# The routing of a fused attention and two-MoE kernel: dummy products, a mask in one step, and the slots' one-hots in small steps on VectorE

## The chip, the cores and the metric

The kernel runs on one core of a Trainium2 chip. The metric is the device time of one execution in microseconds, the median of three runs. One further execution was taken by the hardware profiler; all times below that are read from a view are on its clock.

## The reference

Three stages follow one another:

```python
# 1. attention, 4 x 8 heads, 576 tokens, head size 64
scores = (q @ k.T) / 8
kth = np.partition(scores, -32, axis=-1)[..., -32:-31]
attn = softmax(np.where(scores >= kth, scores, -1e9))
x = (attn @ v) as 2304 x 512
# 2. soft MoE: 8 experts x 4 slots, hidden size 1024
logits = x @ phi
slot_input = softmax(logits, over tokens).T @ x            # 32 x 512
slot_out[e] = relu(slot_input[e] @ w1[e]) @ w2[e]          # 32 x 512
x = softmax(logits, over the 32 slots) @ slot_out          # c @ slot_out
# 3. noisy top-2 MoE: 8 experts, hidden size 1024
noisy = x @ w_gate + log1p(exp(x @ w_noise)) * noise
top2, top2_w = the two largest of noisy, softmax over the two
for e: mask = top2 == e
       out[mask] += top2_w * (relu(x[mask] @ u1[e]) @ u2[e])
```

## The kernel before, in words

The input of the third stage is never formed. A token's row is c, 32 numbers, times slot_out, so each expert's first layer is the token's c times a matrix g = slot_out @ u1[e] of 32 x 1024. g and c are held as two halves each (gh and gl, high and low part), stacked into 128 rows (`stacked_g`, L928).

What the change touches lies between the end of the soft MoE and the ninth of the 64 chunks of the third stage:

- *Logits* (up to L999). c is turned (five transposes on PE, two copies on ACT, the tile ct), and PE forms the logits of both gates from it. Meanwhile it forms g of expert 0 in four steps of `weigh01`.
- *Choice* (L999 to L1047). DVE adds the noise and takes the largest values of each token (MAX8, L1004, 18 of them). Two one-hots oh follow by comparison, and their sum is the mask mb (L1021). From it PE counts, for each token and expert, how many tokens stand before (`before` and onesb, L1027 and L1030). Between the mask and these, L1024 takes the high half of g from its sum on PE, so that ACT can read the low half (L1039). `gates` (L1044 to L1047) makes the weights of the two experts, puts them into RW, rows of 36 numbers (c, the token's id, the gate), and has SP write RW to DRAM: the transfer xd (L1048).
- *Compaction* (L1133 to L1170). Expert 0's tokens are gathered by PE: 18 one-hots wx, each made by DVE (L1143) or by two steps of ACT (L1140, L1141), times c. The steps of `weigh01` for expert 1 stand between these products. The result is cts.
- *Addresses* (L1072 to L1078). For each token its two places in the eight experts' lists: a partition and a column, pc.
- *Slots* (`spread`, L1084 on, and `rows_of_slots`). The lists are turned round by products of one-hots: 36 of 128 wide for the partitions (the tiles y) and 36 of 40 wide for the columns (eq, times ctn into cx and rr, and times pn). The partitions' one-hots of the first 24 are made by a subtraction on POOL (`far`, L1090) and by Abs and Relu on ACT (`near`, L1094, L1095), and those of the last 12 by DVE (`same`, L1099). 36 products on PE (L1120) give ridx, for every place of a list the row of xd, 40 numbers on each of 128 partitions.
- *Gathers.* By ridx POOL fetches an expert's rows out of xd (`rows`, L1218, five indirect transfers of 128 rows each). `ids_of` (L1223) takes the ids from them, `slots` (L1229 to L1231) and `turn` (L1237) make cts of the expert.
- *Chunks* (`gated`). Chunk n = 8e + c is an eighth of expert e's hidden size. `first(n)` is PE's product g times cts (L1249), its relu as a high half hh on ACT (L1254) and a low half hl on DVE (L1255). `split(n)` makes the halves wh and wl of u2 (L1262, L1265). `second(n)` is, for each of five groups of 128 tokens, three products into one bank (L1273 hh by wh, L1274 hh by wl, L1275 hl by wh). After chunk 7 of an expert `store` scales the five banks by the gate and POOL adds them into the output (L1286).

All engines take their instructions in the order in which the code issues them. Chunk n's loop body is: split(n+2), two groups of second(n), first(n+2), the other three groups, and then the extras of `if n == ...`. `later` (before chunk 8) folds a flag over the partitions, which tells whether the fast path may be trusted; its transposes are L697. SP issues the weights' transfers in one queue, as buffers come free. tb, gp, tl and t2 are pools of memory: tb (with RW in it) is given back before tl (the tiles hl) and t2 (the one-hots, cx, xs) are opened, and the memory of tl and t2 is laid out again over what came free.

Of the kernel before, what the change touches and what calls it, by code (L numbers as in the profile page):

```python
# [40 lines left out]
def moe_after_topk_attention(ctx: ExitStack, tc: tile.TileContext, q, k, v, phi, w1, w2, wg, wn, noise, u1, u2, qk, vt, out):  # L41
# [740 lines left out]
    def moe(st, xp, xs, fast):  # L782
# [26 lines left out]
        def warm(n):  # L809

            p = bank("acc0")
            for _ in range(n):
                T.matmul(p, onesb, onesb.unsqueeze(1).to_broadcast([128, 4, 128]), start=True, stop=True)
# [89 lines left out]
        ct = tb.tile([128, 5, 128], F32, name="ct")  # L903
        cf = cn.rearrange("p t s -> p (t s)")
        pc = [bank(x) for x in ("acc3", "acc2")]
        for g in range(4):
            T.transpose(pc[0][:, g * 128:g * 128 + 128], cf[:, g * 128:g * 128 + 128], identf)
        T.transpose(pc[1][:64, :128], cf[:, 512:576], identf)
# [45 lines left out]
        def halve1(e, p):  # L954
            for x, h, _ in quarters(e, p):
                A.copy(h, x)
            for x, h, l in quarters(e, p):
                V.tensor_tensor(l, x, h, op=OP.subtract)
# [58 lines left out]
        oh = gp.tile([128, 2, TT, 8], F32, name="oh")  # L1017
        V.tensor_tensor(oh, ng.unsqueeze(1).to_broadcast([128, 2, TT, 8]),
                        m8[:, :, 0:2].rearrange("p t c -> p c t").unsqueeze(3).to_broadcast([128, 2, TT, 8]), op=OP.is_equal)
        mb = small("mb", BF)  # L1020
        V.tensor_tensor(mb, oh[:, 0], oh[:, 1], op=OP.add)  # L1021
        V.tensor_tensor(gw[:, 1], m8[:, :, 1], m8[:, :, 0], op=OP.subtract)
        for r, (x, h, _) in enumerate(quarters(0, P0)):
            T.matmul(x, minus, h.bitcast(F32), start=False, stop=True, tile_position=(0, 32 * r), skip_group_check=True)  # L1024
# [8 lines left out]
        T.matmul(tot[:, :144], onesb, mbf, start=True, stop=True)  # L1033
        tots = SM
# [6 lines left out]
        A.activation(gw[:, 1], gw[:, 1], AF.Exp)  # L1041
# [38 lines left out]
        def spread(t2):  # L1080
# [6 lines left out]
            eq = t2.tile([128, 36, m], BF, name="eq", bufs=1)  # L1087
# [27 lines left out]
            return pairs, far, near, same, columns, partitions  # L1115
# [74 lines left out]
        gated(st, ps, halves, tw, gather, cts0, done, first_weights, halve1, keep_g, stacked_g, GSS, begin, later,  # L1190
# [3 lines left out]
    def gated(st, ps, halves, tw, gather, cts0, done, first_weights, halve1, keep_g, stacked_g, GSS, begin, later,  # L1194
# [107 lines left out]
        for n in range(8 * E):  # L1302
# [6 lines left out]
            if n < 8 * E - 4:  # L1309
# [3 lines left out]
                if n == 2:  # L1313
                    rows_of_slots(ps.tile([128, 512], F32, name="tp"), pairs)
# [47 lines left out]
            if e + 1 < E:  # L1362
                if c == 1 and e + 1 != 4:
# [154 lines left out]
```

## Time and profile before

| | |
|---|---|
| median of three runs | 760.02 us (758.58 to 761.44) |
| the profiled execution | 757.91 us, its span 756.1 us |
| mean granted clock of PE | 0.982 |
| busy: PE, its weight loads, DVE, ACT, POOL | 727.9, 602.4, 556.5, 489.0, 505.2 us |
| chain that ended last, by engine | PE 51%, DVE 25%, POOL 11%, issue 6%, DMA 4% |
| moved by DMA | 135.22 MB |

The span is the time from the first to the last instruction of the profiled execution; its own time lies 1.8 us above that. The attention fills the first half, with all engines busy. From about 450 us to the end PE is the busiest engine. The routing lies between 455 and 530 us.

### The profile page before, as it was taken

To read this page: it belongs to the slowest core of one execution; us is meant where nothing else is said; L and a number is where in the kernel's file an instruction comes from. 1 tells how busy PE (TensorE), PEld (TensorE's weight loads), DVE (VectorE), ACT (ScalarE), POOL (GpSimd) and SP (SyncE) were. 2 spreads that over 40 slices of the span, in tenths; PEclk is the share of its full clock that TensorE was granted. 3 is DMA by queue.
4 is the path that set the end of the run, shared out by engine and by line. 5 is a ranking of instruction groups with operands and counts; after the bars stand their busy time and mean duration, and the time that the engine had idled before them with its cause. 6 is when DMAs were issued, how large, how long until landed. Compare 5 with 4: busy or idle time off the path is not lost.

```text
span 756.1 us, 17319 instructions
## 1 busy us (share of the span) xinstructions
PE 727.9 (96%) x5654; PEld 602.4 (80%) x5654; DVE 556.5 (74%) x2632; ACT 489.0 (65%) x1025; POOL 505.2 (67%) x639
## 2 busy tenths in 40 slices
PE   9899999999999999999999997979999999999995
PEld 5799999898999889998889434657885888888884
DVE  7799999999999998999984414856654555555551
ACT  5799999999999999999997204634222222322221
POOL 5999999998999999999775030354742337254044
PEclk9899999999999999999999999989999999999999
DMA  7257869775776634463468699969783987245045
GB/s 210 70 129 212 229 175 241 192 219 159 214 219 186 156 107 105 105 156 74 112 235 300 218 379 395 301 231 322 175 185 92 335 249 146 44 68 74 2 64 70
DMA packets 63286, 135.22 MB, mean 179 GB/s; under 512 B 13650, under 2 KB 14290, under 8 KB 63186
## 3 DMA queue, kind: packets, MB, share of 16 engines
q1 hardware_dynamic: 56146, 123.84, 54.6%
q0 software_dynamic: 7040, 10.18, 9.8%
q8 instruction: 46, 0.75, 0.4%
q14 instruction: 54, 0.44, 0.2%
HBM read 84.37 MB, written 17.97 MB: 135 GB/s over the span
## 4 chain that ended last, share of the span: by engine, by line
PE 51%; DVE 25%; POOL 11%; issue 6%; DMA 4%; ACT 1%; SPq 0%; POOLq 0%; ACTq 0%
DVE c L498 10%; PE acc L1275 9%; PE acc L1273 9%; PE acc L1274 9%; POOL u L521 5%; PE av L562 5%; DVE TH L529 5%; DVE c L505 4%; PE S L462 3%; POOL s L536 3%; PE hp L1249 2%; PE st L541 2%; DMA wx<-in_moe_w_dram 2%; DVE mx L501 2%; PE acc L827 2%
## 5 line engine op out<-in xcount | busy, mean ns | idle before, releaser
L498 DVE MAX8 c<-s 128x8 f32<-128x82 f32 (+1 forms) x1008 | 227.0, 235 | 4.3 <-ACT s L478 3.2
L521 POOL TENSOR_TENSOR u<-g,s 128x576 f32<-128x576 bf16 x144 | 186.5, 1295 | 0.5 <-ACT g L515 0.5
L562 PE MATMUL av<-vb,et 128*128 128x65 f32 (+1 forms) x1600 | 172.3, 262 | 0.8 <-ACT et L548 0.8
L562 PEld LDWEIGHTS av<-vb,et 128*128 128x128 f32 (+1 forms) x1600 | 165.7, 180 | 7.8 <-issue 5.3
L1286 POOL DMA_INDIRECT out_dram<-y,ii x40 | 64.7, 1618 | 122.2 <-ACT y L1285 60.7
L1254 ACT ACTIVATE hh<-hp 128x640 fp32r<-128x640 f32 x62 | 43.8, 707 | 137.4 <-PE hp L1249 128.3
L1275 PE MATMUL acc<-wh,hl 128*128 128x512 f32 x320 | 127.0, 397 | 0.7 <-DVE hl L1255 0.7
L1273 PE MATMUL acc<-wh,hh 128*128 128x512 f32 x320 | 127.4, 398 | 0.0
L1274 PE MATMUL acc<-wl,hh 128*128 128x512 f32 x320 | 126.6, 395 | 0.0
L529 DVE MAX8 TH<-u 128x8 f32<-128x584 f32 x144 | 109.8, 763 | 18.8 <-POOL u L522 17.8
L536 POOL TENSOR_SCALAR s<-s,mx 128x576 f32<-128x576 f32 x144 | 108.1, 751 | 22.4 <-ACT a L535 13.6
L541 PE MATMUL st<-identf,s 128*128 128x128 f32 x576 | 116.3, 282 | 4.4 <-POOL s L536 3.9
L1255 DVE SCALAR_TENSOR_TENSOR hl<-hp,hh 128x640 fp32r<-128x640 f32 x62 | 51.1, 824 | 92.1 <-ACT hh L1254 86.7
L535 ACT ACTIVATE a<-s,TH 128x576 bf16<-128x576 f32 x144 | 117.5, 816 | 0.2
L515 ACT ACTIVATE g<-s,T 128x576 bf16<-128x576 f32 x144 | 116.6, 810 | 0.5 <-POOL u L521 0.5
L462 PE MATMUL S<-ks,qs 128*128 128x288 f32 x600 | 113.0, 314 | 0.0
L542 PE MATMUL st<-steep,a 128*128 128x128 bf16 x576 | 106.5, 220 | 0.0
L480 ACT ACTIVATE s<-S 128x576 f32<-128x576 f32 x141 | 97.0, 688 | 6.6 <-PE S L469 4.6
L541 PEld LDWEIGHTS st<-identf,s 128*128 128x128 f32 x576 | 84.3, 146 | 13.5 <-POOL s L536 6.5
L553 ACT ACTIVATE et<-st 128x512 f32<-128x512 f32 x144 | 90.4, 628 | 5.6 <-PE st L542 4.9
L462 PEld LDWEIGHTS S<-ks,qs 128*128 128x128 f32 x600 | 84.7, 190 | 2.0
L1275 PEld LDWEIGHTS acc<-wh,hl 128*128 128x128 f32 x320 | 60.6, 189 | 14.4 <-DVE hl L1255 1.2
(337 smaller groups left out, 1155.5 us busy)
## 6 DMA issues: line engine op xcount, KB each, us to landing
wa<-in_moe_w_dram SPq DMA_DIRECT2D x8, 2048.0 KB
wa<-in_moe_w_dram SPq DMA_DIRECT2D x28, 512.0 KB
wb<-in_moe_w_dram SPq DMA_DIRECT2D x5, 2048.0 KB
ks<-hl SPq DMA_DIRECT2D x60, 160.0 KB
ks<-raw SPq DMA_DIRECT2D x60, 160.0 KB
raw<-in_qk_dram SPq DMA_DIRECT2D x15, 608.0 KB
wy<-in_moe_w_dram SPq DMA_DIRECT2D x4, 2048.0 KB
wb<-in_moe_w_dram SPq DMA_DIRECT2D x16, 512.0 KB
```

Of the source, the lines that this page charges most:

```text
L462: T.matmul(ph[hf][:, :288], QS[h][:, q0:q0 + 128], KS[h][:, l, ks], start=(n == 0), stop=(n == len(mm) - 1))
L498: V.max(C[i][:, c * 8:c * 8 + 8], SS[i][:, cut[c]:cut[c + 1]])
L515: A.activation(g, SS[i], AF.Sign, bias=last8(T24, i, 1), scale=-OVER, accum_out=SM[:, i:i + 1])
L521: G.tensor_tensor(u[:, 0:S], G1[i], SS[i], op=OP.mult)
L529: V.max(last8(TH, i), UU[i])
L535: A.activation(AP[i // 2][:, S * (i % 2):S * (i % 2) + S], SS[i], AF.Relu, bias=last8(TH, i, 1), scale=-1.0)
L536: G.tensor_scalar(SS[i], SS[i], -1.0, MX[i][:, 0:1], op0=OP.mult, op1=OP.add)
L541: T.matmul(o, SP[i // 2][:, ks], identf, start=True, stop=True, is_transpose=True)
L562: T.matmul(av[h][o:o + m, tt * 65:tt * 65 + 65], x, VB[j % 2][:, h, c if c < 4 else 4 + i % 2], start=(c == 0), stop=(c == 4), tile_positi ...
L1273: T.matmul(ACC[j], HH[n][:, r], WH[n], start=(c == 0), stop=False)
L1274: T.matmul(ACC[j], HH[n][:, r], WL[n], start=False, stop=False)
L1275: T.matmul(ACC[j], HL[n][:, r], WH[n], start=False, stop=(c == 7))
```

## The change

The edits, in the order of the code:

- `turn_c` forms ct inside the loop over the experts of the soft MoE, before its last expert, not after the loop.
- Six products with no use (`warm(6, "acc2")`) follow the four steps of `weigh01(0)`.
- mb is one comparison with the second largest value, ahead of oh. The products of L1024 stand behind the counts.
- `gates` runs after the compaction. `addresses` runs in chunk 0, not ahead of it.
- The one-hots y of tokens 0 to 15 and 24 to 35 are 28 steps of DVE, each 128 x 128 on a 16-bit ramp ntb; those of tokens 16 to 23 are nine steps of ACT. ctn has a number for each place of eq and is 16-bit, and the product with it runs on DVE. POOL makes none of these. They are spread over chunks 0, 1 and 2.
- `rows_of_slots`, `rows(1)` and `ids_of(1)` stand after chunk 3 (before: within and after chunk 2), `first_weights2` after chunk 4 (before: chunk 3). The stacked g of expert 1 is written at chunk 3, not 1.
- `keep_tie`, three small steps of DVE ahead of the flag's fold in `later`, marks a tie of the two largest values.
- Some tiles are padded, so that the buffers behind them start elsewhere.

```diff
@@ the soft MoE's loop
             if e == E - 2:
+                turn_c()
                 A.copy(sos, sx)
@@ the logits
                 weigh01(0, c, P0)
+            warm(6, "acc2")
@@ the choice
+        V.tensor_tensor(mb, ng, m8[:, :, 1:2].to_broadcast([128, TT, 8]), op=OP.is_ge)
         V.tensor_tensor(oh, ...)
-        V.tensor_tensor(mb, oh[:, 0], oh[:, 1], op=OP.add)
-        V.tensor_tensor(gw[:, 1], m8[:, :, 1], m8[:, :, 0], op=OP.subtract)
-        for r, (x, h, _) in enumerate(quarters(0, P0)):
-            T.matmul(x, minus, h.bitcast(F32), start=False, stop=True, ...)
+        V.tensor_tensor(below, m8[:, :, 1], m8[:, :, 0], op=OP.subtract)
...
         T.matmul(tot[:, :144], onesb, mbf, start=True, stop=True)
+        for r, (x, h, _) in enumerate(quarters(0, P0)):
+            T.matmul(x, minus, h.bitcast(F32), start=False, stop=True, ...)
@@ the one-hots
-        ctn = gp.tile([128, 2 * TT], F32, name="ctn")
+        ctn = gp.tile([128, 2 * TT, E * JT], BF, name="ctn")
+        ntb = gp.tile([128, 128], BF, name="ntb")
...
-            def far(k):
-                G.tensor_tensor(lt[k], nt[:, 0:128].unsqueeze(1).to_broadcast([128, 8, 128]),
-                                pc[:, 0, 8 * k:8 * k + 8].unsqueeze(2).to_broadcast([128, 8, 128]), op=OP.subtract)
+            def far(a, b):
+                for i in range(a, b):
+                    V.tensor_scalar(lt[i // 8][:, i % 8], ntb, pc[:, 0, i:i + 1], None, op0=OP.is_equal)
             def near(k):
-                A.activation(lt[k], lt[k], AF.Abs)
+                for i in range(8):
+                    A.activation(lt[k][:, i], ntb, AF.Abs, bias=pc[:, 0, 8 * k + i:8 * k + i + 1], scale=-1.0)
                 A.activation(lt[k], lt[k], AF.Relu, bias=1.0, scale=-1.0)
...
-                    G.tensor_tensor(x[:, :, 0], eq[:, a:a + n], ctn[:, a:a + n].unsqueeze(2).to_broadcast([128, n, m]),
-                                    op=OP.mult)
+                    V.tensor_tensor(x[:, :, 0], eq[:, a:a + n], ctn[:, a:a + n], op=OP.mult)
@@ the compaction
-        for n, c in zip((3, 3, 3, 3), range(4)):
+        for n, c in zip((0, 3, 3, 3), range(4)):
             some(n)
             weigh01(1, c, P1)
...
-        some(2)
-        gates()
         some(TT)
@@ the flag
+        def keep_tie():
+            tie = gp.tile([128, 1], F32, name="tie")
+            V.tensor_reduce(tie, below, op=OP.max, axis=AX.X)
+            V.tensor_scalar(tie, tie, 0.0, None, op0=OP.is_lt)
+            V.tensor_tensor(sure, sure, tie, op=OP.mult)
         def later(t2):
+            keep_tie()
@@ the chunks
         gather()
-        addresses()
+        gates()
         done()
...
             if n == 0:
-                begin()
-                for k in range(3):
-                    far(k)
-                    near(k)
+                halve1(1, P1, False)
+                addresses()
                 columns()
                 partitions()
-                for k in range(3, 5):
-                    same(k)
+            if n == 1:
+                near(2)
+                far(0, 16)
             if n == 2:
+                far(24, 2 * TT)
+                halve1(1, P1, True)
+            if n == 3:
+                rows_of_slots(ps.tile([128, 512], F32, name="tp"), pairs)
                 rows(1)
                 ids_of(1)
-            if n == 3:
+            if n == 4:
                 first_weights2(ps.tile([128, 512], F32, name="tp"))
-            if n == 4:
                 slots(1)
                 rows(0)
```

How the instructions stand, at three places. Names: acc, hp and tp are banks of sums, gw the two gates, cts and hl as above, RW the rows that xd writes, zs the flag's tile. "waits" names the semaphores on which an instruction waits, by engine or by the lane of the transfers (DMAHW4 is a lane of SP's). A number behind a name is that of the buffer.

The first place is DVE, from the end of the compaction to the first hl. Before, where L1044 to L1047 stand ahead of three one-hots of the compaction (not shown), and L1072 to L1078 behind it:

```order
L1047 COPY RW<-gw 128x36 [waits DVE_49]
...
L1170 CAST cts_8730<-acc_8648 64x320 [waits PE_49]
L1170 CAST cts_8730<-acc_8648 64x320
L1072 TENSOR_TENSOR oh<-oh,pe 128x288 [waits DVE_49]
...
L1078 TENSOR_SCALAR pc<-ia 128x72 [waits DVE_49]
L1255 SCALAR_TENSOR_TENSOR hl<-acc_8761,hh 128x320 [waits Activation_49]
L1255 SCALAR_TENSOR_TENSOR hl<-acc_8762,hh 128x320 [waits Activation_49]
```

And now:

```order
L1172 CAST cts_8734<-acc_8657 64x320 [waits PE_49]
L1172 CAST cts_8734<-acc_8657 64x320
L1051 TENSOR_SCALAR gw<-gw 128x18
L1052 RECIPROCAL gw<-gw 128x18 [waits DVE_49]
L1053 TENSOR_TENSOR gw<-gw 128x18 [waits DVE_49]
L1054 COPY RW<-gw 128x36 [waits DVE_49]
L1262 SCALAR_TENSOR_TENSOR hl<-acc_8764,hh 128x320 [waits DMAHW4_49,DVE_49,Activation_49]
L1262 SCALAR_TENSOR_TENSOR hl<-acc_8765,hh 128x320 [waits Activation_49]
L1272 TENSOR_TENSOR wl<-wa_8447,wh 128x512 [waits Activation_49]
```

The gates moved behind the copies of cts, the addresses went to chunk 0, and the first hl has a wait on DMAHW4, the lane of xd, which it did not have. Before, the first to wait for that lane was POOL, in the first of these rows of its own queue; of them only the gathers of L1218 are left on POOL now:

```order
L1090 TENSOR_TENSOR y<-nt,pc 128x1024 [waits DMAHW0_49,DVE_49,DMAHW4_49,PE_49,DMAHW7_49,Activation_49,Pool_49]
L1090 TENSOR_TENSOR y<-nt,pc 128x1024 x2
L1106 TENSOR_TENSOR cx<-eq,ctn 128x16x40 [waits DVE_49,Pool_49]
L1106 TENSOR_TENSOR rr<-eq,ctn 128x20x40 [waits DVE_49]
L1218 DMA xs<-xd,ridx 128x36 [waits DVE_49]
```

The second place is ACT in chunks 0 to 2. Before:

```order
L1254 ACTIVATE hh<-hp 128x640 [waits PE_49]
L956 CAST gh_8512<-tp 32x256 x4
L1094 ACTIVATE y<-y 128x1024 [waits DMAHW4_49,Pool_49]
L1095 ACTIVATE y<-y 128x1024 [waits Activation_49]
...
L1111 ACTIVATE cx<-eq,pn 128x16x40 [waits DVE_49]
L1111 ACTIVATE rr<-eq,pn 128x20x40 [waits DVE_49]
L1262 CAST wh<-wa_8446 128x512
L1254 ACTIVATE hh<-hp 128x640 [waits PE_49]
```

And now:

```order
L1261 ACTIVATE hh<-hp 128x640 [waits PE_49]
L963 CAST gh_8511<-tp 32x256 x4
L1115 ACTIVATE cx<-eq,pn 128x16x40 [waits DVE_49,DMAHW4_49,Activation_49,Pool_49]
L1115 ACTIVATE rr<-eq,pn 128x20x40 [waits DVE_49]
L1269 CAST wh<-wa_8447 128x512
L1261 ACTIVATE hh<-hp 128x640 [waits PE_49]
L1104 ACTIVATE y<-ntb,pc 128x128 x8
L1105 ACTIVATE y<-y 128x1024 [waits Activation_49]
L1269 CAST wh<-wa_8447 128x512 [waits DMAHW5_49]
```

The six large steps on y went; the steps on eq now stand first, and eight small ones and one large one stand a chunk later.

The third place is PE before chunk 8, where the flag is folded. Before:

```order
L1274 MATMUL acc_8812<-wl,hh 128x512
L1275 MATMUL acc_8812<-wh,hl 128x512
L697 MATMUL tp<-identf,zs 1x128
L1273 MATMUL acc_9212<-wh,hh 128x512 [waits Activation_49]
L1274 MATMUL acc_9212<-wl,hh 128x512
```

And now:

```order
L1281 MATMUL acc_8815<-wl,hh 128x512
L1282 MATMUL acc_8815<-wh,hl 128x512
L697 MATMUL tp<-identf,zs 1x128 [waits DVE_49]
L1280 MATMUL acc_9251<-wh,hh 128x512 [waits Activation_49]
L1281 MATMUL acc_9251<-wl,hh 128x512
```

L697 stands where it stood, and now waits for DVE, on whose queue the steps of `keep_tie` come after the two products y of the store of chunk 7.

## Rows read from the trace of the kernel before

**Rows 1.** Windows: PE, PEld, DVE, ACT, POOL busy (count), PEclk, DMA share, GB/s

```profile
469.00:471.00 2.00, 1.21 (x4) 0.60 (x4) 2.00 (x6) 1.94 (x5) 0.00 (x0) 0.58 1.05 387
476.00:476.50 0.50, 0.50 (x7) 0.21 (x9) 0.50 (x2) 0.00 (x0) 0.00 (x0) 0.84 0.99 246
```

**Rows 2.** Timeline of PE: start, duration (us), instruction, [idle before it <- released by]

```profile
467.10 0.63 PE L1024 MATMUL acc<-gh,minus 32*32 32x256 f32 x8 [1.61 <-ACT gh L1015]
...
470.52 0.58 PE L1147 MATMUL acc<-wx,xw 128*64 128x320 f32 x2 [0.63 <-ACT wx L1141]
...
481.28 1.06 PE L1249 MATMUL acc<-cts,gs 128*128 128x320 f32 x4 [0.79 <-ACT cts L1169]
...
483.69 0.50 PE L1275 MATMUL acc<-wh,hl 128*128 128x512 f32 x1 [0.74 <-DVE hl L1255]
...
494.50 0.73 PE L1120 MATMUL tp<-cx,y 128*128 128x80 bf16 x16 [2.18 <-issue]
...
506.69 0.62 PE L1205 MATMUL tp<-wa,soT 128*32 128x512 f32 x1
...
510.26 0.50 PE L1273 MATMUL acc<-wh,hh 128*128 128x512 f32 x1
...
517.85 0.60 PE L1237 MATMUL tp<-identf,cx 128*128 128x128 f32 x4
...
526.90 0.38 PE L697 MATMUL tp<-identf,zs 128*1 128x128 f32 x2
```

**Rows 3.** Timeline of SP's queue, issues of transfers

```profile
470.56 0.53 SPq L132 DMA_DIRECT2D wa<-in_moe_w_dram  x1
477.56 0.35 SPq L1048 DMA_DIRECT2D xd<-RW  x1
```

**Rows 4.** POOL's line L1090: duration min/median/max (ns), first and last start (us)

```profile
L1090 POOLq EVENT_SEMAPHORE  x3: 43/43/25372, 457.9 to 484.3; - x3
```

**Rows 5.** Timeline of POOL

```profile
499.54 1.26 POOL L1218 DMA_INDIRECT xs<-xd,ridx  x1 [3.81 <-DVE ridx L1126]
...
508.13 0.19 POOL L1223 CAST ii<-xs 128x5 int32<-128x5 f32 x1 [2.09 <-DMA xs<-xd,ridx]
...
521.66 0.19 POOL L1223 CAST ii<-xs 128x5 int32<-128x5 f32 x1 [6.58 <-DMA xs<-xd,ridx]
```

**Rows 6.** Timeline of DVE

```profile
465.38 1.32 DVE L1004 MAX8 nz<-T 128x8 f32<-128x8 f32 x18
...
481.54 0.46 DVE L1072 TENSOR_TENSOR oh<-oh,pe 128x288 f32<-128x288 f32 x1
...
483.04 0.20 DVE L1078 TENSOR_SCALAR pc<-ia 128x72 f32<-128x72 int32 x1
483.16 0.88 DVE L1255 SCALAR_TENSOR_TENSOR hl<-acc,hh 128x320 fp32r<-128x320 f32 x2
...
486.86 0.81 DVE L1255 SCALAR_TENSOR_TENSOR hl<-hp,hh 128x640 fp32r<-128x640 f32 x1
...
515.16 0.36 DVE L1231 CAST cx<-cx 128x320 fp32r<-128x320 f32 x1
...
526.40 1.40 DVE L1283 TENSOR_SCALAR y<-acc,xs 128x512 f32<-128x512 f32 x2
```

**Rows 7.** Groups of DVE by form, 420 to 520 us: busy us, mean ns | idle

```profile
L958 DVE TENSOR_TENSOR gl<-tp,gh 32x256 fp32r<-32x256 f32 x4 | 1.7, 420 | 0.1
L1104 DVE TENSOR_TENSOR eq<-nt,pc 128x800 bf16<-128x800 f32 x1 | 1.0, 979 | 0.0
```

**Rows 8.** Groups of ACT by form, the same stretch

```profile
L1262 ACT CAST wh<-wa 128x512 fp32r<-128x512 f32 x8 | 4.9, 614 | 0.0
L1254 ACT ACTIVATE hh<-hp 128x640 fp32r<-128x640 f32 x6 | 4.2, 705 | 10.1 <-PE hp L1249 10.0
L1095 ACT ACTIVATE y<-y 128x1024 bf16<-128x1024 bf16 x3 | 3.2, 1058 | 0.1
```

**Rows 9.** Group of DVE by form, whole span

```profile
L64 DVE TENSOR_SCALAR before<-jp 128x128 bf16<-128x128 int32 x1 | 0.2, 223 | 0.0
```

More of the change, by code (lines that the diff above doesn't have):

```diff
@@ L807, in moe, with warm @@
         more(20)
-        def warm(n):
-            p = bank("acc0")
+        def warm(n, name="acc0"):
+            p = bank(name)
             for _ in range(n):
@@ L879, in moe, with turn_c @@
                             op0=OP.max)
+        ct = tb.tile([128, 5, 128], F32, name="ct")
+        def turn_c():
+            cf = cn.rearrange("p t s -> p (t s)")
+            x = halves()
+            for g in range(4):
+                T.transpose(x[:, 0, g * 128:g * 128 + 128], cf[:, g * 128:g * 128 + 128], identf)
+            T.transpose(x[:64, 1, :128], cf[:, 512:576], identf)
+            A.copy(ct[:, 0:4], x[:, 0].rearrange("p (a b) -> p a b", a=4))
+            A.copy(ct[:64, 4], x[:64, 1, :128])
         sx, so = bank("acc2"), [bank(f"acc{n}") for n in range(2)]
@@ L902, in moe @@
             more(19 if fast else 20)
[L903 to L908, printed above, removed]
         p = fold_t(sos, 4, fold)
-        A.copy(ct[:, 0:4], pc[0].rearrange("p (a b) -> p a b", a=4))
-        A.copy(ct[:64, 4], pc[1][:64, :128])
         ta_st.close()
         gp = pool("gp", 1, st)
-        soT = gp.tile([128, 4, NS], F32, name="soT")
+        soT = gp.tile([128, 4 * NS + 24], F32, name="soT")[:, 0:4 * NS].rearrange("p (c s) -> p c s", s=NS)
         V.tensor_copy(soT, p)
@@ L952, in quarters, with halve1 @@
                     for r in range(4)]
-        def halve1(e, p):
-            for x, h, _ in quarters(e, p):
-                A.copy(h, x)
+        def halve1(e, p, lo):
             for x, h, l in quarters(e, p):
-                V.tensor_tensor(l, x, h, op=OP.subtract)
+                if lo:
+                    V.tensor_tensor(l, x, h, op=OP.subtract)
+                else:
+                    A.copy(h, x)
         def keep_g(g):
@@ L1017, in moe @@
         oh = gp.tile([128, 2, TT, 8], F32, name="oh")
+        mb = small("mb", BF)
+        V.tensor_tensor(mb, ng, m8[:, :, 1:2].to_broadcast([128, TT, 8]), op=OP.is_ge)
         V.tensor_tensor(oh, ng.unsqueeze(1).to_broadcast([128, 2, TT, 8]),
                         m8[:, :, 0:2].rearrange("p t c -> p c t").unsqueeze(3).to_broadcast([128, 2, TT, 8]), op=OP.is_equal)
-        mb = small("mb", BF)
-        V.tensor_tensor(mb, oh[:, 0], oh[:, 1], op=OP.add)
-        V.tensor_tensor(gw[:, 1], m8[:, :, 1], m8[:, :, 0], op=OP.subtract)
-        for r, (x, h, _) in enumerate(quarters(0, P0)):
-            T.matmul(x, minus, h.bitcast(F32), start=False, stop=True, tile_position=(0, 32 * r), skip_group_check=True)
+        below = gp.tile([128, TT], F32, name="below")
+        V.tensor_tensor(below, m8[:, :, 1], m8[:, :, 0], op=OP.subtract)
         pos = bank("acc3")
@@ L1033, in moe @@
         T.matmul(tot[:, :144], onesb, mbf, start=True, stop=True)
+        for r, (x, h, _) in enumerate(quarters(0, P0)):
+            T.matmul(x, minus, h.bitcast(F32), start=False, stop=True, tile_position=(0, 32 * r), skip_group_check=True)
         tots = SM
@@ L1040, in moe @@
         stacked_g(0)
-        A.activation(gw[:, 1], gw[:, 1], AF.Exp)
+        A.activation(gw[:, 1], below, AF.Exp)
         def gates():
@@ L1114, in spread @@
             pairs = [(lt[i // 8][:, i % 8], r[i]) for i in range(2 * TT)]
-            return pairs, far, near, same, columns, partitions
+            return pairs, far, near, columns, partitions
         def rows_of_slots(p, pairs):
@@ L1189, in done, with gated @@
             xs.close()
-        gated(st, ps, halves, tw, gather, cts0, done, first_weights, halve1, keep_g, stacked_g, GSS, begin, later,
+        gated(st, ps, halves, tw, gather, cts0, done, first_weights, halve1, keep_g, stacked_g, GSS, P1, gates, later,
               addresses, spread, rows_of_slots, ridx, soT, gh, gl)
-    def gated(st, ps, halves, tw, gather, cts0, done, first_weights, halve1, keep_g, stacked_g, GSS, begin, later,
+    def gated(st, ps, halves, tw, gather, cts0, done, first_weights, halve1, keep_g, stacked_g, GSS, P1, gates, later,
               addresses, spread, rows_of_slots, ridx, soT, gh, gl):
@@ L1294, in gated @@
         gather()
-        addresses()
+        gates()
         done()
         tl, t2 = pool("tl", 4, st), pool("t2", 2, st)
-        pairs, far, near, same, columns, partitions = spread(t2)
+        pairs, far, near, columns, partitions = spread(t2)
         first(0)
@@ L1312, in gated @@
                 second(n, range(2))
-                if n == 2:
-                    rows_of_slots(ps.tile([128, 512], F32, name="tp"), pairs)
                 if m < 8 * E:
@@ L1362, in gated @@
             if e + 1 < E:
-                if c == 1 and e + 1 != 4:
+                if c == (1 if e else 3) and e + 1 != 4:
                     stacked_g(e + 1)
```

13 lines of the change are left out of this document (4 added, 9 removed).

## Prediction

> **What bounds the kernel now.** I read the windows by stage first, then PE's timeline around the routing, then SP, POOL and DVE in the same stretch. The change begins near 456 us, and after the opening of the gated stage it adds one wait, at chunk 8. [...] First(0), the opening of the gated stage, starts at 481.28 after a wait for ACT's copy, and its hl product then waits 0.74 us for DVE [rows 2]. From there PE is the pace, but for the hole of 2.18 us before L1120 (rows_of_slots, 494.50); chunk 3 ends where L1205 (first_weights2) begins, at 506.69 [rows 2].
>
> One time is not written in any row and decides the sum: when the transfer xd, issued at 477.56 behind the 2 MB weight of 470.56 [rows 3], lands. POOL's first L1090 waits for DVE's pc and for the semaphore that xd raises (its row in the order is [waits DMAHW0_49, DVE_49, DMAHW4_49, ...]). Of its three wait instructions the first begins at 457.9 and takes 25.37 us, that is, to 483.3, where pc is ready (483.04 + 0.20) [rows 4, 6]; the last begins only at 484.3 [rows 4]. The 0.9 us between are a wait for a transfer. I read xd's landing as 484.2, 6.6 us after its issue.
>
> **Part by part.**
>
> *Logits turned in the w2 stage.* Five transposes and two copies go ahead of the last expert's products, where PE waits for a weight anyway. The fold after them still needs DVE's second add. I take 0.3 us gained (0 to 0.5).
>
> *Mask in one step, dummy products, gates later.* mb is ready 0.5 us earlier, since oh (as large as L1072's step of 0.46 [rows 6]) no longer stands ahead. But L1024's four products move behind the prefix products, so ACT's low halves and with them its first one-hot come 0.6 us later; PE meets that one-hot at 471.1 instead of 470.5 [rows 2]. If the six dummy products hold the clock, the 5.7 us from there to 476.2 that ran at half clock [rows 1] shrink by half, 2.9. One of four weigh01 steps now stands in the hole before that one-hot, 0.6 less. Sum: 2.9 + 0.6 - 0.6 + 0.3 = 3.2 us, first(0) at 478.1 for 481.28. Bounds: 0.3 if the clock falls all the same, 4.
>
> *The wait that is added.* The order shows what the diff hides: with the larger ctn the pool of hl lies over the memory of RW, and hl's first product on DVE now waits for DMAHW4, xd's semaphore. Gates stand right before it: four steps, 0.9 us, after the cts copies that end at 478.1. So xd is issued near 479.3, two us later than now, and still queues behind the weight that 484.2 already allowed for: it lands at 484.2 to 484.3 again. Queued behind the waiting DVE instruction are both hl, both wl, addresses, columns, everything. PE runs out after first(0), first(1) and two products, stands from 479.5 to 484.8, and starts the first L1282 at 484.85 where it now starts L1275 at 483.69 [rows 2]. The 3.2 us are gone, and 1.1 more. Bounds for the landing: 481.6 (issue plus the 2.1 us that POOL waits from its last gather to ii [rows 5], nothing queued ahead) and 486.0 (issue plus today's 6.6). I take 484.3.
>
> *The one-hots.* From 484.3 the chain is DVE's and ACT's, not PE's:
> - hl(0) to the end of hl(2): 483.16 to 487.67 now, 4.5 us [rows 6]. POOL no longer runs beside it, but PE at half clock delays first(2); I keep 4.4: 488.7.
> - addresses, 481.54 to 483.24, 1.7 [rows 6]: 490.4.
> - columns on DVE: eq of 800 took 0.98 [rows 7], so eq of 640 takes 0.8. The product with ctn, new on DVE, is not in the trace: as long as eq (0.8) at most, half that at least; between the two eq stands 0.7: 0.8 + 0.7 + 0.9 = 2.4, to 492.8.
> - ACT's partitions 0.95 (a 1024-wide step is 1.06 [rows 8]), wh 0.61, hh 0.70 [rows 8]: 495.0. wh(3) stands behind the partitions on ACT.
> - near: eight steps of 128 at 0.27 (on the line through 0.61 for 512 and 1.06 for 1024 [rows 8]) and one of 1.06, 3.2; then wh(4), hh(4), 1.3; hl(4) 0.75: 500.25. The 16 small steps of far lie beside near on DVE.
> - the 12 small steps of far(24, 36): between 0.073 (18 MAX8 in 1.32 [rows 6]) and 0.223 each (a 128x128 step into 16 bits alone, L64 [rows 9]); I take 0.11, 1.3 us. Then the low halves, 4 x 0.42 [rows 7], which hold the bank that rows_of_slots writes: 503.3.
> - rows_of_slots, 36 products in 1.6 (the first 16 take 0.73 [rows 2]): chunk 4 can start at 504.95.
>
> [...]
>
> Now chunk 3 ends at 506.69 with rows_of_slots behind it already; after, the same place is 504.95: 1.75 us gained. Chunk 4 and first_weights2 cost the same in either order.
>
> *Behind it.* ridx is ready at 506.0, now 499.4: POOL's five gathers take 6.5 (499.54 to 506.04, which is 508.13 less the wait of 2.09 [rows 5]), to 512.5, and land as now 2.1 us later, 514.6. slots(1) is three small DVE steps, the largest 0.36 [rows 6], some 1.0; turn(1) can stand near 515.9, and PE wants it at 516.1 (517.85 [rows 2] less 1.75). No loss, no slack.
>
> *keep_tie.* Three small DVE steps behind the two y of chunk 7, 0.6 us, and L697's product on PE, which waits for nothing now, then waits for them. y begins at 526.40 and takes 1.40, so L697 could start at 528.4 on this clock, where it now stands at 526.90 [rows 2, 6]: 1.5 us lost. What this adds to DVE later in chunk 8 lies in its slack. The offsets of the buffers I put at nothing, bounded by 0.5 either way.
>
> **Sum.** -1.75 + 1.5 = -0.25 us, rounded -0.3. Against the profiled execution, 757.9 us (span 756.1), that is 757.6; the median of the runs lies 2.1 above the profiled one, so 759.7. Its own range, from the bounds of the unknown costs, is 757 to 762.5.
>
> **Rivals.**
> - *xd doesn't hold hl*: it lands at 481.6, before the weight is through, and the chain starts 2.7 us earlier: 757.0. If hl is not held at all, hl(0) starts at 479 and PE sets the pace again: rows_of_slots ends near 499.5, 5.5 us earlier: 754.2. [...] Against: the 6.6 us of the present run, with the weight issued before it. I call the case 754.5.
> - *The gathers come too late* (slower): the place is POOL's fifth gather at 512.5 against the 2 MB weight that SP issues as soon as first_weights2 ends: 504.95, a chunk (3.8, half of 510.26 to 517.85) and its own 3.6 (506.69 to 510.26 [rows 2]), 512.3. In the present run ii waits 6.58 us behind the last gather of rows(0) [rows 5], as I read it because weights stand beside it, where rows(1) took 2.09. If the weight wins, rows(1) lands 2 to 3 us later, at 517.2, and turn(1) at 518.5; rows(0) is whole 13.5 us behind ii (508.13 to 521.66 [rows 5]), so at 530.7, its fourth piece two gathers sooner, 528.3, DVE's y ends at 529.0, tie at 529.6, and L697 stands 2.8 us later than now: 762.8; with small steps at 0.223, 764.2. It decides from one us of further delay of ridx. For it: ridx loses 6.6 us against today, PE gains only 1.75. Against: rows(0) has slack now (521.66 against y at 526.40 [rows 5, 6]).
> - *The clock falls in the compaction too*: then first(0) is at 481.0 (the 0.3 alone), gates end at 482, xd is issued behind them and lands near 486: 1.7 later, 761.4. [...]
>
> **Chances.** Forecast 0.55; xd not in the way 0.15; gathers late 0.20; clock 0.10. What a measurement of this kernel can tell from no change is about 0.5%, 3.8 us: faster is below 756.2, slower above 763.8. Faster: most of the first rival and a little of the forecast's edge, 0.17. Slower: the gathers with dear small steps or together with the clock, 0.18. Same 0.65. The range for 8 in 10 is 754.5 to 764.
>
> **What would show it.** Right: first(0) near 478; DVE idle before the first L1262 until 484, released by a transfer; PE idle some 5 us there and half clock behind it; no POOL work beside DVE; rows_of_slots at 503 to 505; L697 idle before it, released by DVE. Wrong: L1282's first product before 482, rows_of_slots before 500, or POOL's ii waiting beyond 517.

## The result and the profile after

The changed kernel takes 767.08 us (median of 6, 765.26 to 769.88), the kernel before in the same comparison 760.79: a ratio of 1.0094 by the comparison (95% interval 1.0071 to 1.0118; the two medians alone give 1.0083). That is slower, beyond what the measurement leaves open, and outside the range of 754.5 to 764 that was given.

The profiled execution after has a span of 768.1 us, 12.0 more than before, but not all of that is the change's. Ahead of the first edit both timelines have 48 products of the soft MoE's second layer, L890 before and L901 after. PE's timeline of the kernel before, and then of the changed one:

```profile
444.49 5.36 PE L890 MATMUL acc<-wy,wb 128*32 128x512 f32 x48
```

```profile
447.89 5.36 PE L901 MATMUL acc<-wy,wb 128*32 128x512 f32 x48
...
470.66 0.22 PE L1032 MATMUL acc<-mb,before 128*128 128x144 bf16 x1 [0.21 <-DVE mb L1025]
...
474.92 0.39 PE L1151 MATMUL acc<-wx,xw 128*64 128x320 f32 x2 [1.90 <-ACT wx L1145]
...
483.98 1.05 PE L1256 MATMUL acc<-cts,gs 128*128 128x320 f32 x4 [0.79 <-ACT cts L1171]
...
489.76 0.77 PE L1282 MATMUL acc<-wh,hl 128*128 128x512 f32 x1 [4.10 <-DVE hl L1262]
...
509.27 0.73 PE L1124 MATMUL tp<-cx,y 128*128 128x80 bf16 x16 [1.04 <-DVE gl L961]
...
527.26 1.09 PE L1244 MATMUL tp<-identf,cx 128*128 128x128 f32 x4 [5.23 <-DVE cx L1238]
...
540.38 0.38 PE L697 MATMUL tp<-identf,zs 128*1 128x128 f32 x2 [1.39 <-DVE zs L1179]
```

The two executions are 3.40 us apart there already, ahead of the first edit. In the profiles of the twelve experiments below, whose code is the same up to there, this row begins between 443.0 and 446.0, so the 3.40 is taken as spread of the executions. So a time of the changed profile less 3.40 is compared with [rows 2], and the change's share of the span is the stretch from this row to the end: 311.6 us before, 320.2 after, 8.6 more. The medians are only 6.3 apart: the profiled execution after is the slowest of its six, and the one before (757.91) is below all six of the kernel before. On that footing first(0) starts at 480.58 for 481.28, rows_of_slots at 505.87, turn(1) at 523.86 for 517.85, and L697 at 536.98 for 526.90, 10.1 later. Three holes of PE are new: 4.10 us ahead of the first hl product, 5.23 ahead of turn(1), 1.39 ahead of L697.

What released them is on the other engines. DVE, SP and POOL of the changed kernel, where [rows 6, 3, 5] were:

```profile
489.02 0.89 DVE L1262 SCALAR_TENSOR_TENSOR hl<-acc,hh 128x320 fp32r<-128x320 f32 x2 [3.85 <-DMA xd<-RW]
...
500.91 2.69 DVE L1100 TENSOR_SCALAR y<-ntb,pc 128x128 bf16<-128x128 bf16 x16
...
526.11 0.26 DVE L1236 CAST cx<-xs 128x160 fp32r<-128x160 f32 x1 [5.30 <-DMA xs<-xd,ridx]
...
538.46 1.40 DVE L1290 TENSOR_SCALAR y<-acc,xs 128x512 f32<-128x512 f32 x2
539.78 0.16 DVE L1177 TENSOR_REDUCE tie<-below 128x1 f32<-128x18 f32 x1
```

```profile
474.95 0.53 SPq L132 DMA_DIRECT2D wa<-in_moe_w_dram  x1
485.23 0.35 SPq L1055 DMA_DIRECT2D xd<-RW  x1
...
510.48 8.05 SPq L132 DMA_DIRECT2D wa<-in_moe_w_dram  x2
519.40 0.36 SPq L967 DMA_DIRECT2D gd<-gh  x1
```

```profile
512.84 1.26 POOL L1225 DMA_INDIRECT xs<-xd,ridx  x1 [58.78 <-PE hp L1256]
...
518.35 1.00 POOL L1225 DMA_INDIRECT xs<-xd,ridx  x1 [0.30 <-issue]
526.14 0.24 POOL L1230 CAST ii<-xs 128x5 int32<-128x5 f32 x1 [6.78 <-DMA xs<-xd,ridx]
```

The first hl waits for xd, as forecast. The ids wait 6.78 us behind the fifth gather, where they waited 2.09 [rows 5]; the second of the two weights of 510.48, which waits for first_weights2, is issued from 518.16 to 518.53, the fifth gather from 518.35, 0.2 us behind it. By the trace's semaphore events the first four gathers have landed by 519.4 us and the fifth at 526.0.

The clock, by windows of the changed kernel (columns as in [rows 1]):

```profile
472.00:474.00 2.00, 1.01 (x14) 0.35 (x10) 2.00 (x6) 1.77 (x6) 0.00 (x0) 1.00 1.05 387
476.00:478.00 2.00, 2.00 (x14) 1.16 (x14) 0.92 (x2) 1.94 (x3) 0.00 (x0) 0.50 1.09 183
484.00:486.00 2.00, 1.66 (x6) 0.91 (x6) 1.03 (x5) 1.57 (x5) 0.00 (x0) 1.00 0.34 133
490.00:492.00 2.00, 2.00 (x6) 1.63 (x7) 1.90 (x4) 0.00 (x0) 0.00 (x0) 0.50 1.02 397
528.00:530.00 2.00, 1.32 (x5) 0.88 (x4) 1.59 (x3) 0.85 (x2) 1.45 (x2) 0.50 1.02 408
```

The granted clock fell to half three times: to 0.50 in the window from 476, in the compaction, behind the hole of 1.90 us, later than before (0.58 from 469 [rows 1]); to 0.50 from 490, with the hole of 4.10; and to 0.50 from 528, with that of 5.23. The row from 484 shows the DMA engines only 0.34 busy about the place where xd is issued.

### The profile page after: what moved, and what is told of

Its sections match the earlier page's. It is cut to its first block, busy times and chain, and to the rows that moved or that the text cites. A ratio compares the mean times of both kernels' runs of the same rounds, so it can differ in the third digit from the quotient of the medians.

```text
span 768.1 us, 17366 instructions
## 1 busy us (share of the span) xinstructions
PE 730.8 (95%) x5660; PEld 607.2 (79%) x5660; DVE 557.6 (73%) x2663; ACT 487.3 (63%) x1028; POOL 499.4 (65%) x635
## 4 chain that ended last, share of the span: by engine, by line
PE 50%; DVE 21%; POOL 13%; issue 7%; DMA 5%; ACT 3%; POOLq 0%; SPq 0%; DVEq 0%; ACTq 0%
PE acc L1282 8%; PE acc L1280 8%; PE acc L1281 8%; DVE c L498 7%; PE av L562 6%; POOL u L521 5%; DVE TH L529 4%; PE S L462 4%; POOL s L536 3%; PE st L541 3%; DVE c L505 3%; DMA wx<-in_moe_w_dram 3%; PE hp L1256 2%; DVE mx L501 2%; POOL raw L433 2%
## 5 line engine op out<-in xcount | busy, mean ns | idle before, releaser
L498 DVE MAX8 c<-s 128x8 f32<-128x82 f32 (+1 forms) x1008 | 222.6, 230 | 5.5 <-ACT s L478 3.1
L521 POOL TENSOR_TENSOR u<-g,s 128x576 f32<-128x576 bf16 x144 | 189.1, 1313 | 0.3 <-ACT g L515 0.3
L562 PE MATMUL av<-vb,et 128*128 128x65 f32 (+1 forms) x1600 | 174.5, 264 | 0.9 <-ACT et L548 0.9
L562 PEld LDWEIGHTS av<-vb,et 128*128 128x128 f32 (+1 forms) x1600 | 168.0, 182 | 7.8 <-issue 5.3
L1293 POOL DMA_INDIRECT out_dram<-y,ii x40 | 65.2, 1630 | 112.4 <-issue 57.5
L536 POOL TENSOR_SCALAR s<-s,mx 128x576 f32<-128x576 f32 x144 | 111.1, 772 | 26.4 <-ACT a L535 13.8
L1225 POOL DMA_INDIRECT xs<-xd,ridx x40 | 44.3, 1108 | 70.4 <-PE hp L1256 58.8
```

Of the source, the lines that this page charges most:

```text
L498: V.max(C[i][:, c * 8:c * 8 + 8], SS[i][:, cut[c]:cut[c + 1]])
L521: G.tensor_tensor(u[:, 0:S], G1[i], SS[i], op=OP.mult)
L536: G.tensor_scalar(SS[i], SS[i], -1.0, MX[i][:, 0:1], op0=OP.mult, op1=OP.add)
L562: T.matmul(av[h][o:o + m, tt * 65:tt * 65 + 65], x, VB[j % 2][:, h, c if c < 4 else 4 + i % 2], start=(c == 0), stop=(c == 4), tile_positi ...
```

## The experiments

Each run is the changed kernel with the edit shown. The last two columns are from its profile, in us: from the start of the 48 products of L901 (before: L890) to first(0), and to the end of the span.

| run | median us | ratio to before (95%) | to first(0) | to the end |
|---|---|---|---|---|
| before | 759.6 to 760.8 | 1 | 36.8 | 311.6 |
| changed | 767.08 | 1.0094 (1.0071 to 1.0118) | 36.1 | 320.2 |
| e1 stacked g later | 766.33 | 1.0100 (1.0064 to 1.0136) | 36.0 | 319.6 |
| e2 hl free of xd | 762.11 | 1.0034 (1.0020 to 1.0049) | 37.6 | 314.1 |
| e3 no dummies | 768.12 | 1.0105 (1.0075 to 1.0135) | 39.2 | 322.8 |
| e4 e1, e2, keep_tie early | 760.35 | 1.0011 (0.9994 to 1.0028) | 37.4 | 313.7 |
| e5 first_weights2 later | 764.06 | 1.0062 (1.0043 to 1.0081) | 36.4 | 316.8 |
| e6 e1, e2, e5, keep_tie early | 760.14 | 1.0004 (0.9980 to 1.0027) | 37.6 | 312.5 |
| e7 gates early | 766.59 | 1.0089 (1.0059 to 1.0118) | 37.2 | 319.2 |
| e8 large one-hot steps | 766.93 | 1.0094 (1.0067 to 1.0122) | 37.2 | 320.4 |
| e9 e2, e5, keep_tie early, turns later | 755.41 | 0.9941 (0.9923 to 0.9959) | 37.3 | 308.2 |
| e10 e9, partitions later | 754.41 | 0.9923 (0.9903 to 0.9942) | 37.7 | 307.6 |
| e11 e5 with turns later | 761.71 | 1.0021 (1.0000 to 1.0041) | 37.0 | 314.0 |
| e12 e10, no dummies | 752.56 | 0.9898 (0.9877 to 0.9920) | 37.1 | 307.1 |

**e1, the stacked g later.** The first theory on the late gathers blamed the weight of 510.48, which stood in SP's queue behind transfers that wait for the low halves.

```diff
-                if c == (1 if e else 3) and e + 1 != 4:
+                if c == (1 if e else 5) and e + 1 != 4:
```

> The changed kernel, but expert 1's stacked g is written out at chunk 5 and not at chunk 3, so that SP issues the next 2 MB weight ahead of the transfers that wait for the low halves. Theory 1 (the weight waits in SP's queue behind the low halves, leaves at 510.5 us and runs beside the gathers): the weight leaves near 497, the ids of expert 1 wait some 2 us behind the last gather for 6.78, the hole before turn(1) falls from 5.2 us to under 1, the time to 760 (757 to 762). Theory 2 (ridx is late, and the gathers are as slow without the weight): the wait stays over 5 us, the time at 767. Theory 3 (the wait for xd at the opening is the whole loss, and passes to the end): 767.

SP and POOL of e1:

```profile
483.90 0.45 SPq L132 DMA_DIRECT2D wa<-in_moe_w_dram  x1
...
513.36 0.37 SPq L132 DMA_DIRECT2D wa<-in_moe_w_dram  x1
```

```profile
513.55 1.00 POOL L1225 DMA_INDIRECT xs<-xd,ridx  x1 [0.30 <-issue]
521.22 0.24 POOL L1230 CAST ii<-xs 128x5 int32<-128x5 f32 x1 [6.67 <-DMA xs<-xd,ridx]
```

That weight now leaves at 483.90 and nothing is gained: theory 1 was wrong in which weight it blamed. The other one, behind first_weights2, still leaves 0.2 us before the fifth gather.

**e2, hl free of xd.** ctn moves from the pool gp to t2, so that hl ends below RW's old pool.

```diff
-        ctn = gp.tile([128, 2 * TT, E * JT], BF, name="ctn")
+            ctn = t2.tile([128, 2 * TT, E * JT], BF, name="ctn", bufs=1)
```

> The changed kernel, but ctn lies in the pool of the one-hots, so that the tiles hl end below the memory of RW and the first hl does not wait for xd. Theory 3 (the wait for xd at the opening passes to the end): hl(0) comes 3.9 us sooner, no half clock behind it, the time 763 or less. Theory 1 (the collision at the gathers is the greater part): the same 3 to 4 us at the opening, but the ids still wait 6 us or more and the hole before turn(1) stays near 5 us: 763 to 764, not 760. If the hold costs nothing because the hole takes it up: 767.

hl(0) starts right behind the gates, at 483.93, and PE has no hole and no half clock at the first hl product (the granted clock is 1.00 from 484 to 488); 5.0 us less in the medians, 6.1 in the profiles. The wait was a loss that passed to the end. PE at turn(1) still stands 3.56 us, and the ids wait 5.71. Here the fifth gather is issued at 512.27 and the weight behind first_weights2 at 512.68, so the gather is late with the weight 0.4 us behind it, too. Counted from the 48 products (445.27 here) and put on the clock of before, that gather is at 511.5, one us ahead of the 512.5 of the prediction.

**e3, no dummies.** The line `warm(6, "acc2")` is left out.

> The changed kernel without the six dummy products. If they hold PE's clock (full from 470 to 475 us in the changed profile): half clock comes some 3 to 5 us sooner, first(0) 1 to 2 us later, the time 768 to 769. If the clock falls in the hole before ACT's first one-hot whatever was done before: first(0) in place within 0.5 us, 767.

PE's clock in e3:

```profile
464.00:466.00 2.00, 2.00 (x17) 1.36 (x20) 0.44 (x2) 0.74 (x3) 0.00 (x0) 0.50 1.05 416
476.00:478.00 2.00, 2.00 (x13) 0.67 (x12) 1.11 (x2) 1.57 (x3) 0.00 (x0) 0.50 0.97 385
```

It falls twice, and first(0) is 3.1 us later than in the changed profile. But the first fall, ahead of the dummies' place, stands in profiles with the dummies too, and the second comes there at times: e2 falls once (0.50 from 464 to 470, 1.00 from 472 to 482), e9 and e10 twice (both 0.57 from 464 to 468, then 0.72 and 0.77 from 476 to 480). The medians are 1.0 apart, within their intervals.

**e4, three edits.** e1 and e2, and keep_tie in chunk 0.

```diff
                 halve1(1, P1, False)
+                keep_tie()
                 addresses()
```

> The changed kernel with the edits of the two runs above (the stacked g at chunk 5, ctn in the pool of the one-hots) and the three steps of keep_tie in chunk 0 rather than ahead of the flag's fold. Theory 1 with the wait for xd and L697's hole as separate losses that add up: 767 less 7, 4 and 1.4, near 755 (752 to 758), faster than the kernel before. Theory 2: 762. If the losses cover one another: 758 to 760.

The hole at L697 is gone; the one at turn(1), 4.50 us, is not. 760.35 and not 755: the ids still wait 6.57 us, with the weight issued at 512.46, 0.46 behind the fifth gather, and e1's edit does nothing for that.

**e5, first_weights2 later.** Now the other weight.

```diff
             if n == 4:
-                first_weights2(ps.tile([128, 512], F32, name="tp"))
                 slots(1)
...
             if n == 5:
+                first_weights2(ps.tile([128, 512], F32, name="tp"))
                 turn(1, 0, 4)
```

> The changed kernel, but first_weights2 stands in chunk 5, ahead of turn(1), and not in chunk 4, so that the 2 MB weight which waits for it leaves SP 3.7 us later, behind the fifth gather of expert 1. Theory 1 as it now stands (only the fifth gather is late, because that weight and the two gd transfers are issued as it is; the first four land before 519.4 us in the changed profile): the ids wait some 2 us for 6.78, the hole before turn(1) falls from 5.2 us to under 1, no half clock behind it: 760 (758 to 762). Theory 2 (the last gather is as late without the weight): the wait stays near 6.7, 767.

POOL and PE of e5:

```profile
517.70 0.24 POOL L1230 CAST ii<-xs 128x5 int32<-128x5 f32 x1 [2.01 <-DMA xs<-xd,ridx]
```

```profile
521.58 0.63 PE L1244 MATMUL tp<-identf,cx 128*128 128x128 f32 x4 [3.42 <-DVE gl L1218]
```

The wait is 2.01 us, as in the kernel before: the collision was with this weight, which here leaves at 518.20, 3.5 us behind the fifth gather, or with the gd transfers behind it; they moved together, and the two were not separated. Theory 2 falls. Of the 7 us that were expected only 3.0 came; part was given back by my edit itself: turn(1) uses the bank out of which DVE still takes first_weights2's low halves.

**e6, three mends.** e2, e5 and keep_tie in chunk 0. The kernel that ran also has e1's edit (the stacked g at chunk 5), which the expectation does not name.

> The changed kernel with first_weights2 in chunk 5, ctn in the pool of the one-hots (hl free of xd) and keep_tie in chunk 0. If the three losses are separate: 762.1 of the run with hl free, less 3.6 for its hole before turn(1), 1.5 for the half clock behind that, 1.4 for L697: 755.5 (753 to 758), faster than the kernel before. If chunk 4's and 5's new order only moves the collision to the gathers of expert 0, and the store then waits: 759 to 761.

760.14. The ids wait 2.01 us, but turn(1) stands 2.83 for the same bank.

**e7, gates early.** The call of `gates` stands where it stood before, in the compaction.

> The changed kernel with the gates where they were, among the compaction's one-hots; hl still lies over RW and waits for xd. If xd lands by the time of its issue (3.8 us in the changed profile): it lands some 4 us sooner, hl is hardly held, 762 to 763 as with hl free. If xd lands when the 2 MB weight ahead of it in the queue is through: it lands 1 to 2 us sooner only, and hl is still held 2 to 3 us: 765.

SP and DVE of e7:

```profile
477.78 0.35 SPq L1055 DMA_DIRECT2D xd<-RW  x1
```

```profile
486.14 0.89 DVE L1264 SCALAR_TENSOR_TENSOR hl<-acc,hh 128x320 fp32r<-128x320 f32 x2 [3.35 <-DMA xd<-RW]
```

Counted from L901 (445.33 here), xd is issued 32.5 us on, 4.9 sooner than in the changed kernel, and hl starts 40.8 on against 41.1, 0.3 sooner; the medians are level. That looks like the second reading, but the weight ahead of xd left later here, too, so the run did not change the issue of xd alone. The profiles with rows of both issues in which hl, or POOL before, waits for xd, in us from the 48 products (before: to the landing of [rows 4]; e1 and e3: hl's start taken as 0.74 us ahead of its first product on PE, as in the changed profile):

| run | weight issued | xd issued | hl starts | hl behind xd |
|---|---|---|---|---|
| before | 26.1 | 33.1 | 39.7 | 6.6 |
| e7 | 29.7 | 32.5 | 40.8 | 8.4 |
| changed | 27.1 | 37.3 | 41.1 | 3.8 |
| e1 | 26.9 | 37.2 | 41.2 | 4.0 |
| e3 | 28.8 | 40.4 | 44.2 | 3.8 |
| e8 | 29.7 | 38.5 | 42.3 | 3.8 |

With the gates late, hl follows xd's issue by 3.8 to 4.0 us, while it stands 12.7 to 15.4 behind the weight's. In e3 the DMA engines moved nothing when xd was issued (the last two columns of the windows):

```profile
482.00:484.00 2.00, 1.33 (x10) 0.94 (x8) 1.96 (x6) 0.76 (x2) 0.00 (x0) 1.00 0.00 0
484.00:486.00 2.00, 1.67 (x6) 0.93 (x6) 1.17 (x5) 1.50 (x5) 0.00 (x0) 1.00 0.00 0
```

```profile
485.37 0.35 SPq L1054 DMA_DIRECT2D xd<-RW  x1
```

So in the changed kernel the landing went by the issue of xd, and not by the weight. Only where xd is issued sooner behind the weight, 2.8 us in e7 and 7.0 before, it took longer, 8.4 and 6.6. Against e8, whose weight left at the same place, e7's issue is 6.0 us sooner and its hl 1.5. Moving the gates back did not free hl, and its worth for the time stays open; what moved the time was to take hl off RW (e2).

**e8, large steps.** `far` makes eight one-hots in one step, by broadcast.

```diff
-                for i in range(a, b):
-                    V.tensor_scalar(lt[i // 8][:, i % 8], ntb, pc[:, 0, i:i + 1], None, op0=OP.is_equal)
+                for i in range(a, b, 8):
+                    n = min(8, b - i)
+                    V.tensor_tensor(lt[i // 8][:, 0:n], nt[:, 0:128].unsqueeze(1).to_broadcast([128, n, 128]),
+                                    pc[:, 0, i:i + n].unsqueeze(2).to_broadcast([128, n, 128]), op=OP.is_equal)
```

> The changed kernel with the 28 small steps of the one-hots as four large ones (three of 1024 columns, one of 512, read by broadcast). If the fixed part of a step is what small steps cost (28 at 0.168 us are 4.7 us; large ones by the 0.98 us for 800 columns of eq are 4.4): the chain 0.3 us shorter, 767. If small 16-bit steps are the faster form (large ones with POOL idle as slow as the 2.28 us for 1024 columns of the kernel before): the chain 3 to 4 us longer, 769 to 771.

DVE's groups by form in e8 (busy us, mean ns):

```profile
L1101 DVE TENSOR_TENSOR y<-nt,pc 128x1024 bf16<-128x1024 f32 x3 | 3.6, 1217 | 0.0
L1101 DVE TENSOR_TENSOR y<-nt,pc 128x512 bf16<-128x512 f32 x1 | 0.7, 684 | 0.0
```

Its timeline has 2.35 and 1.82 us for the two groups, 4.17 together, where the small steps took 2.69 and 2.04, 4.73. The small 16-bit steps are no faster; the time is the same.

**e9, turns later.** e6 without e1's edit, and with both turns of expert 1 behind all products of chunk 6.

```diff
-                if n == 6:
-                    turn(1, 4, JT)
                 second(n, range(2))
+                if n == 6:
+                    second(n, range(2, JT))
+                    turn(1, 0, 4)
+                    turn(1, 4, JT)
                 if m < 8 * E:
                     first(m)
-                second(n, range(2, JT))
+                if n != 6:
+                    second(n, range(2, JT))
...
             if n == 5:
                 first_weights2(ps.tile([128, 512], F32, name="tp"))
-                turn(1, 0, 4)
```

> The run with three mends again (hl free, keep_tie in chunk 0, first_weights2 in chunk 5), with both turns of expert 1 behind all products of chunk 6, so that turn(1) does not wait for the bank that first_weights2 leaves to its low halves (2.8 us in that run). If that hole and the half clock behind it were what kept it from 755.5: 760.1 less 2.8 and less 1.5: 756 (754 to 757.5). If the end is set elsewhere by then (the gathers of expert 0 beside the weight): 759 to 760.

No hole of more than 0.7 us is left between rows_of_slots and the end of chunk 8, and the granted clock is full from 480 to 552 us: 755.41, faster than the kernel before, by 0.6%. Against e6 two things differ; e11 has the turns alone.

**e10, partitions later.** In e9, `partitions()` moves from chunk 0 to chunk 1.

> The run with the turns behind chunk 6, and ACT's two steps for the partitions (0.83 and 0.96 us) behind split(3) and first(3), in chunk 1. If the chain of the one-hots sets when rows_of_slots starts: DVE no longer waits 0.93 us for ACT's wh(3), PE's hole before first(4) (2.5 us) shrinks to about 1, rows_of_slots 0.9 us sooner: 755. If PE's work behind it has slack for that: 756, as without.

PE's hole before first(4) is 1.39 us for 2.52, and rows_of_slots starts 57.5 us behind L901's start for 58.2. 754.41; the intervals of e9 and e10 overlap.

**e11, turns alone.** e5 with e9's place of the turns.

> The changed kernel with first_weights2 in chunk 5 and both turns behind chunk 6, and nothing else (hl still waits for xd, keep_tie where it was). If the losses add up: 767.1 less the hole of 5.2 and the half clock behind it, 1.7: 760 (759 to 761.5), level with the kernel before; the rest to 755.4 is hl's wait and L697's. If hl's wait covers part of it: 762 or more.

6.2 us less than the changed kernel in the profiles, 5.4 in the medians; against e5, which differs by the turns alone, 2.8 and 2.4. With e2's 6.1 and 5.0 that is 12.3 and 10.4, and e9, which has both and keep_tie early, is 12.0 and 11.7 less: the losses at hl and at the turns add up to within some 1.5 us. What keep_tie's hole alone is worth at the end was not tested.

**e12, e10 without the dummies.**

> The fastest run (hl free, keep_tie in chunk 0, first_weights2 in chunk 5, both turns behind chunk 6, the partitions in chunk 1) without the six dummy products. If they save PE a second fall of its clock in the compaction (first(0) came 3.1 us later without them in the profiles of the changed kernel) and nothing covers it here: 757 to 757.5. If what they cost and what they hold are level: 754.4.

Neither reading: 752.56. But the profiles differ by 0.5 us from L901 on, first(0) by 0.6, the clock falls twice ahead of first(0) in both (to 0.57 and 0.77 in windows of e10, to 0.50 and 0.64 in windows of e12), and the intervals overlap. What the dummies are worth stays open within some 2 us either way; a gain of 3 they are not. This is the fastest version run.

## Why the prediction was wrong

Its forecast, -0.3 us, failed at one step above all: that the five gathers "land as now 2.1 us later". The forecast itself had the weight issued at 512.3, 0.2 us ahead of the fifth gather at 512.5, and the sum gave this no price; measured on the common clock they stand at 514.8 and 515.0, again 0.2 apart, and the ids wait 6.78 us. e5, with that weight 3.5 us behind the gather, has 2.01 again. The terms in their order:

- *Logits.* 0.3 gained was forecast; the first product behind the fold, 464.94 (L981) for 461.32 (L976) before, is 0.2 later on the common clock.
- *Mask and dummies.* mb is 0.3 sooner (467.23 before, 470.30 after; 0.5 forecast), the second one-hot 1.0 later (0.6). The clock did fall in the compaction, and first(0) gained 0.7 for 3.2. The forecast held that the dummies would keep the clock. Its 2.9 for that is half of the 5.7 us up to 476.2, where the 0.84 of [rows 1] puts the turn back to full; no run shows that the dummies save it: with them the clock fell to 0.50 all the same, and without them first(0) came 3.1 us later in e3 than in the changed kernel, and 0.6 sooner in e12 than in e10. The hole before ACT's one-hot, 0.63 us in [rows 2], is 1.90 now that L1040 stands late; behind it the clock fell. The price came through xd: the gates stand behind the copies of cts, and with first(0) 2.5 us later than forecast xd was issued 2.5 later, at 481.8 for 479.3.
- *The wait that is added.* Right in kind: hl was held by xd. Wrong in what sets the landing: the forecast had it from the weight ahead, as before, and the table at e7 shows it 3.8 us behind xd's own issue. It landed at 485.6 on the clock of before for 484.3 forecast. That is what the third rival (the clock falls in the compaction) had said: first(0) at 481.0, xd near 486, with a chance of 0.10. The rival that xd doesn't hold hl is out.
- *The one-hots.* From hl(0) to rows_of_slots 20.25 us, 19.0 forecast. Most of the difference is the small steps: 0.168 us each, 0.11 taken, 0.7 for the twelve on the path. Another 0.5 is hl(2), which ended 4.9 us behind the start of hl(0), 4.4 taken. An ACT step took 0.30 for 0.27. The products with ctn were 0.49 and 0.57, inside their bounds. Together with xd, rows_of_slots came at 505.87 for 503.3, and the 1.75 gained at the end of chunk 3 became 0.8 lost.
- *The gathers.* The second rival was what happened, at the place that it named: the fifth gather against the weight behind first_weights2. It had a chance of 0.20 and a price of 762.8, and was to decide only from one us of further delay. Both came 2.5 us later than forecast, but it needed no delay: in e2 the gather was one us ahead of the forecast and the ids waited 5.71. The price was too low twice. The fifth gather landed 4.7 us late (6.78 less 2.09), not 2.6, and PE's hole of 5.23 us was followed by half clock: from turn(1) to L697 took 13.12 us, less the hole of 1.39, where it took 9.05, 2.7 more. "No loss, no slack" should have read as a warning: a chain with no slack, 0.2 us from a 2 MB transfer, deserved more than a chance of one in five. The prediction's sign of being wrong there, ii waiting beyond 517, came true: 522.7 on that clock.
- *keep_tie.* 1.5 forecast, 1.39 measured.

At L697 the terms are 0.8 + 5.2 + 2.7 + 1.4 = 10.1 us, what the two timelines differ by. 1.5 of it are gone again by the end of the span; where was not traced.

What many small steps cost against few large ones, the runs show for these one-hots alone: 28 steps of 128 columns took 0.17 us each in the changed kernel, 4.73 in all, and the four large ones of e8 4.17, 0.56 less.

## What to carry to other kernels

Where an edit takes the slack out of a chain that ends in a small transfer, look at which large transfers the queues will issue at that moment: with one issued within half a us of the fifth gather, ahead (changed kernel) or behind (e2, e4), the ids waited 6.78, 5.71 and 6.57 us, and 2.01 with that weight, and the gd transfers that moved with it, 3.5 us behind (e5). The difference, 3.7 to 4.8 us, is more than the whole chain was forecast to gain, 1.75. A larger tile can move the pools behind it over memory that a transfer still reads; the order of the instructions shows the wait, and moving one tile to a later pool took it away (e2, 5.0 us less in the medians). When an edit removes a hole, see what the bank or buffer that it moves past is waiting for: e5 and e6 gave part of their gain to a bank (holes of 3.42 and 2.83 us), which e11 and e9 got back (2.4 and 4.7 us less in the medians).

## What the runs showed of the hardware

- A comparison of 1024 columns by broadcast took DVE 1.22 us with POOL idle (e8). The kernel before ran the same form at 2.28 us beside POOL's large steps, in this group of its DVE by form:

```profile
L1099 DVE TENSOR_TENSOR y<-nt,pc 128x1024 bf16<-128x1024 f32 x1 | 2.3, 2279 | 0.0
```

  It ran from 492.06 to 494.34; POOL's step beside it ended at 493.27, 1.07 us ahead of that end:

```profile
491.39 1.88 POOL L1106 TENSOR_TENSOR cx<-eq,ctn 128x640 bf16<-128x640 bf16 x1 [0.83 <-DVE eq L1104]
493.22 2.51 POOL L1106 TENSOR_TENSOR rr<-eq,ctn 128x800 bf16<-128x800 bf16 x1
```

- The ids waited 5.7 to 6.8 us behind the fifth gather where a 2 MB weight was issued between 0.2 us ahead of it and 0.5 behind (the changed kernel, e1, e2, e3, e4), and 2.0 to 2.1 where it was issued 3.5 and 4.1 us behind (e5, e9). They waited 6.7 in e7 and e8, with first_weights2 in chunk 4, and 2.0 in e6 and e10 to e12, with it in chunk 5.
- xd held hl for 3.8 to 4.0 us from its issue where the weight ahead of it was issued 8.8 us or more before, and for 8.4 where that was 2.8 (e7).
- PE's clock fell once in the compaction in the kernel before (0.50 from 470 to 476) and in the changed one (0.50 from 476 to 478), at different places, and in some profiles ahead of the dummies (e2, 0.50 from 464 to 468; e9, 0.57); first(0) came 36.0 to 37.7 us behind L901 in all runs but e3.
